# One flat query load with full-width transposes, and gated single-buffered loads, in a pooled-attention plus gated-convolution kernel

## The chip, the cores and the metric

The kernel runs on one core of a Trainium2 chip. The metric is the device time of one execution in microseconds (us). The engines that matter are TensorE (PE in the profile; PEld is its loading of stationary operands), VectorE (DVE), ScalarE (ACT), GpSimd (POOL, which also issues the loads that turn float32 into bfloat16) and SyncE (SP, which issues the other transfers). Matmul results go to an accumulator memory, PSUM, which the kernel uses as four slots.

## The reference

There are 8 batches, 8 heads, 576 tokens and 64 values per head. Keys and values are averaged over 8 neighbouring tokens, which leaves 72 of them. Attention runs over those, and a gated feed-forward block follows.

```python
k_p = k.reshape(B, H, 72, 8, 64).mean(axis=3)
v_p = v.reshape(B, H, 72, 8, 64).mean(axis=3)
attn = softmax(q @ k_p.T / 8)              # per head: 576 x 72
x = (attn @ v_p), heads side by side       # B x 576 x 512
h = maximum(x @ w_in, 0)                   # B x 576 x 1024
c = conv_w[0]*h[t-1] + conv_w[1]*h[t] + conv_w[2]*h[t+1]
out = (h * sigmoid(c)) @ w_out             # B x 576 x 512
```

## The kernel before, in words

The order of every engine's instructions is the order in which the program is written: `start()` does the attention of batch 0, and `batch(b)` then mixes the feed-forward work of batch `b` with the attention of batch `b + 1`, in nine pieces `a0` to `a8` that `attention()` returns. A batch's feed-forward is eight blocks of `mm1` (L246, x times a 128-column block of w_in, ReLU on ACT), four of `conv` (L272, 48 small 32x32 matmuls, then tanh on ACT), four of `gate` (L299, DVE), and four or five of `mm2` (L311, 128 tokens of two batches' output).

The attention of a batch has these steps.

- `k_tree` and `v_tree` (L140, L134) sum eight tokens on DVE by three additions. `k_turn` (L151) transposes the pooled keys on PE and DVE copies them out of PSUM.
- `q_prep(b, h0, n)` (L164) turns the queries of four heads. A row of the query tile holds four neighbouring tokens of a head, so that 128 rows hold tokens 0 to 511; the 64 tokens left lie in a second tile `qt` of 16 rows. Each head takes two transposes of 128x128 (L171) whose result is written in four runs of 32 elements, and two of 16 rows (L174). One DVE copy (L180) takes four heads out of PSUM.
- `scores` (L186) is two matmuls of a head and one exponential on ACT (L197). `av` (L205) multiplies 128 tokens of all heads by the values, and DVE divides by the sum (L220, L221).
- `xt` (L229) transposes the result, with `perm` or `perm_last` in place of the identity matrix, so that tokens come out in their natural order, and DVE copies it (L244). `mm1` needs it.

Every `mm1` block but two is also written a second time with its rows turned by 32, 64 or 96 partitions, by two transfers on SP (L269, L270); `gate` reads those copies.

Loads: the first batch's keys come as float32 through SP, everything else through POOL. Key, value and query tiles have two buffers each; `load(b + 2)` stands in the first piece of `batch(b)`. A load into a buffer in use waits on POOL until its readers are done.

## Time and profile before

| | |
|---|---|
| median of 2 runs | 276.54 us (276.31 to 276.78) |
| profiled execution | 276.06 us, of which the span is 274.2 us |
| PE busy | 243.9 us (89% of the span) |
| DVE busy | 158.7 us (58%) |
| ACT busy | 121.2 us (44%) |
| POOL busy | 33.9 us (12%) |
| moved by DMA | 33.87 MB, 124 GB/s on average |

The profiled execution lies 0.48 us below the median. It spends 1.9 us outside the span. A row of the timeline gives a start and a length in us from the span's start. The length of a group of matmuls holds the pipeline's tail, about a sixth to a fifth of a us; the pace of a series is read from the start of one group to the start of the next. "PEclk" is the clock that TensorE was granted: 1.00 is full, 0.50 half.

### The profile page before, as it was taken

The page shows a single profiled execution, that of the slowest core. Times are in us where ns is not written, and L with a number is a line of the kernel's source. Part 1 is how long each engine was busy: PE and PEld are TensorE (multiplying, and loading weights), DVE is VectorE, ACT ScalarE, POOL GpSimd, SP SyncE. Part 2 cuts the span into 40 slices and gives each one's busy share as a digit, 9 for nine tenths or more (in the row PEclk, how much of TensorE's full clock was granted, in tenths as well). Part 3 has the DMA queues.
Part 4 walks back from the last instruction along what each step waited for, and adds up shares of the span by engine and source line. Part 5 has one row for each costly group of instructions (what it writes and reads, how often), then busy time and mean ns, then how long its engine had stood idle before and what let it go on. Part 6 is the DMA issues. An engine that isn't in the chain of part 4 may idle for free.

```text
span 274.2 us, 7517 instructions
## 1 busy us (share of the span) xinstructions
PE 243.9 (89%) x3244; PEld 157.8 (58%) x3265; DVE 158.7 (58%) x295; ACT 121.2 (44%) x209; POOL 33.9 (12%) x56
## 2 busy tenths in 40 slices
PE   0268889789999999999999999999999999999984
PEld 0145557466666656566666666666666666665531
DVE  3564936484579337664579348664876474742341
ACT  1033016705582346514582358434572638265530
POOL 8452343100220022000220021000000000000000
PEclk9999999959999979997999999999999999999999
DMA  6999999993599229942599229521121212324333
GB/s 132 204 196 186 162 164 200 194 171 67 74 196 211 67 42 167 186 130 65 70 191 202 85 41 196 162 79 47 62 82 62 83 60 82 104 67 130 91 114 117
DMA packets 38045, 33.87 MB, mean 124 GB/s; under 512 B 5732, under 2 KB 32828, under 8 KB 38012
## 3 DMA queue, kind: packets, MB, share of 16 engines
q0 software_dynamic: 24512, 15.68, 42.7%
q1 hardware_dynamic: 13500, 17.72, 21.6%
q8 instruction: 25, 0.41, 0.7%
q14 instruction: 8, 0.07, 0.1%
HBM read 32.52 MB, written 9.44 MB: 153 GB/s over the span
## 4 chain that ended last, share of the span: by engine, by line
PE 65%; ACT 14%; DVE 9%; DMA 6%; issue 4%; POOL 0%; DVEq 0%; ACTq 0%; SPq 0%; POOLq 0%
PE o_ps L317 22%; PE h_ps L251 19%; PE q_ps L171 8%; PE q_ps L174 5%; ACT tg L294 4%; ACT attnT L197 4%; PE c_ps L285 4%; DMA qr<-in_q_dram 4%; DVE x L221 3%; DMA hT_108<-hT_108 3%; ACT hT_108 L259 2%; ACT hT_109 L259 2%; PE sc_ps L189 2%; PE xt_ps L237 2%; PE kT_ps L155 1%
## 5 line engine op out<-in xcount | busy, mean ns | idle before, releaser
L251 PE MATMUL h_ps<-xT,w_in_sb 128*128 128x288 bf16 x512 | 78.0, 298 | 3.1 <-DVE x L221 1.2
L317 PE MATMUL o_ps<-w_out_sb,gT 128*128 128x512 bf16 x267 | 65.6, 382 | 2.1 <-DVE gT L304 0.8
L251 PEld LDWEIGHTS <-w_in_sb 128*128 128x128 bf16 x512 | 49.6, 101 | 21.6 <-issue 4.0
L197 ACT ACTIVATE attnT<-sc_ps 72x576 bf16<-72x576 f32 x64 | 37.8, 651 | 28.7 <-PE sc_ps L189 28.7
L317 PEld LDWEIGHTS <-gT 128*128 128x128 bf16 x288 | 28.0, 99 | 30.2 <-DVE gT L304 1.3
L259 ACT ACTIVATE hT_108<-h_ps 128x576 bf16<-128x576 f32 x32 | 21.0, 656 | 45.2 <-PE h_ps L251 45.1
L259 ACT ACTIVATE hT_109<-h_ps 128x576 bf16<-128x576 f32 x32 | 20.9, 654 | 43.5 <-PE h_ps L251 43.4
L294 ACT ACTIVATE tg<-c_ps 128x576 bf16<-128x576 f32 x64 | 38.3, 661 | 0.2 <-PE c_ps L285 0.2
L180 DVE COPY qT<-q_ps 128x1152 bf16<-128x1152 bf16 x16 | 12.1, 758 | 36.3 <-PE q_ps L174 36.3
L171 PE MATMUL q_ps<-ident,qr 128*128 128x128 bf16 x128 | 30.7, 240 | 2.0 <-DMA qr<-in_q_dram 1.7
L221 DVE TENSOR_TENSOR x<-av_ps,r 128x512 bf16<-128x512 f32 x40 | 27.6, 691 | 1.4
L327 DVE COPY o<-o_ps 128x512 f32<-128x512 f32 x20 | 13.8, 692 | 19.2 <-PE o_ps L317 19.2
L174 PE MATMUL q_ps<-ident,qt 16*128 16x16 bf16 x128 | 23.1, 180 | 0.0
L325 ACT COPY o<-o_ps 128x512 f32<-128x512 f32 x16 | 9.4, 585 | 29.7 <-PE o_ps L317 23.1
L285 PEld LDWEIGHTS <-dw 32*32 32x32 bf16 x1536 | 14.0, 88 | 11.0 <-issue 7.3
L174 PEld LDWEIGHTS <-qt 16*128 16x128 bf16 x128 | 11.8, 92 | 11.7 <-issue 2.5
L210 PEld LDWEIGHTS <-attnT 72*128 72x128 bf16 x320 | 13.8, 104 | 5.9 <-DVE x L221 2.2
L117 POOL DMA_DIRECT2D qt<-in_q_dram x8 | 4.4, 556 | 94.2 <-PE q_ps L174 93.1
L171 PEld LDWEIGHTS <-qr 128*128 128x128 bf16 x128 | 12.6, 98 | 4.3 <-DMA qr<-in_q_dram 1.9
L237 PEld LDWEIGHTS <-x 128*128 128x128 bf16 x160 | 12.1, 108 | 5.0 <-DVE x L221 3.4
L189 PE MATMUL sc_ps<-qT,kz_104 128*72 128x288 bf16 x64 | 12.6, 336 | 1.7 <-DVE qT L180 1.7
L220 DVE RECIPROCAL r<-av_ps 128x8 f32<-128x8 f32 x40 | 8.0, 199 | 8.5 <-PE av_ps L210 8.5
(165 smaller groups left out, 224.3 us busy)
## 6 DMA issues: line engine op xcount, KB each, us to landing
out_dram<-o SPq DMA_DIRECT2D x36, 256.0 KB, 3.7
kr<-in_k_dram POOLq DMA_DIRECT2D x7, 576.0 KB, 13.7
vr<-in_v_dram POOLq DMA_DIRECT2D x7, 576.0 KB, 10.5
qr<-in_q_dram POOLq DMA_DIRECT2D x7, 512.0 KB, 6.6
hT_108<-hT_108 SPq DMA_DIRECT2D x16, 108.0 KB, 4.6
hT_109<-hT_109 SPq DMA_DIRECT2D x16, 108.0 KB, 4.7
hT_108<-hT_108 SPq DMA_DIRECT2D x16, 72.0 KB, 3.9
hT_109<-hT_109 SPq DMA_DIRECT2D x16, 72.0 KB, 2.0
```

Source lines behind the costliest of these rows:

```text
L171: nc.tensor.transpose(out=ym[:, f], in_=st[b]["q"][:, h0 + i, f * P:(f + 1) * P], identity=ident)
L174: nc.tensor.transpose(out=yt[:, f], in_=st[b]["qt"][:, h0 + i, f * P:(f + 1) * P], identity=ident[0:TP, 0:TP],)
L189: nc.tensor.matmul(out=ps[0:Sp, c2, 0:SC], lhsT=kz[b % 2][:, h, c2, :], rhs=st[b]["qT"][h], start=True, stop=True,)
L197: nc.scalar.activation(out=at.rearrange("s (m two j) -> s two m j", two=2, j=GRP), in_=ps[0:Sp, :, 0:SC].rearrange("s two (m j) -> s two m ...
L210: nc.tensor.matmul(out=ps[:, h // 4, c:c + D + 1], lhsT=st[b]["at"][h][:, t0:t0 + P], rhs=va[b % 2][:, h, :], start=True, stop=True,)
L221: nc.vector.tensor_tensor(out=x.rearrange("p (g h) d -> p g h d", g=2), in0=y[:, :, :, 0:D], in1=r.unsqueeze(3).to_broadcast([P, 2, 4, D]) ...
L237: nc.tensor.transpose(out=y[:, pr, ii * P:(ii + 1) * P], in_=st[b]["x"][i][:, 2 * pr:2 * pr + 2, :].rearrange("p h d -> p (h d)"), identit ...
L251: nc.tensor.matmul(out=ps[:, c, 0:SC], lhsT=w_in_sb[:, dc, fb * P:(fb + 1) * P], rhs=xT[:, dc, c * SC:(c + 1) * SC], start=(dc == 0), stop ...
L259: nc.scalar.activation(out=row[:, PAD:S + PAD].rearrange("p (c n) -> p c n", c=NS), in_=ps[:, :, 0:SC], func=ACT.Relu, scale=0.5,)
L285: nc.tensor.matmul(out=ps[j // 2][QD * c:QD * (c + 1), j % 2, 0:SC], lhsT=dw[QD * r:QD * (r + 1), kk, g * NQ + j, :], rhs=row[QD * r:QD * ...
L294: nc.scalar.activation(out=tg[:, 2 * i:2 * i + 2, :], in_=ps[i][:, :, 0:SC], func=ACT.Tanh)
L317: nc.tensor.matmul(out=ps[:, 0, :], lhsT=gT[:, fb, j * P:(j + 1) * P], rhs=w_out_sb[:, fb, :], start=(fb == 0), stop=(fb == n_fb - 1),)
```

## The change

- The queries of a batch are one tile of 128 rows: row `h * 16 + g` holds the 36 tokens from `36 * g` on of head `h`, a contiguous piece of the input. One load brings them, and 18 transposes of 128x128, each for two tokens of every row and so for all heads, turn them, nine in each of two PSUM slots. The copy out of PSUM (L165 in the new numbering) sorts them by head, in runs of 16 elements.
- Every head now needs both halves of the transposes, so the scores leave `a1`; `a2`, `a3` and `a4` have three, three and two heads instead of two each.
- Tokens stand in the attention in the order (token in a row, row): the exponential writes runs of 16 elements instead of 32. The transposes in `xt` write their result in 16 runs of 8 elements, and one `perm` serves all tiles.
- Key, value and query tiles have one buffer each. A batch's loads are written just behind the last reader of the batch before: `load_q` behind the second `q_prep`, `load_v` behind `v_tree`, `load_k` behind `k_tree`, through `pool_keys`.
- In `start()` all loads go through POOL. A one-element copy on POOL, `landed(...)`, stands ahead of most of them, and reads what an earlier load brings, so that POOL waits there for that landing. The scores of the first four heads come behind both halves of `q_prep`, and both `v_tree` behind all scores.
- `first_batch()` takes the place of `batch(0)`: four blocks of `mm1` come ahead of the attention of batch 1, and the second half of the convolution of batch 0 is done there and not in `batch(1)`. `batch(1)` has `pool_keys(2)` in its first piece.
- The output tile has 6 buffers instead of 3, the tanh tile 3 instead of 2.

The diff, cut to what the steps below touch:

```diff
-    kv_pool = ctx.enter_context(tc.tile_pool(name="kv", bufs=2))
-    q_pool = ctx.enter_context(tc.tile_pool(name="q", bufs=2))
+    kv_pool = ctx.enter_context(tc.tile_pool(name="kv", bufs=1))
+    q_pool = ctx.enter_context(tc.tile_pool(name="q", bufs=1))
...
-    tg_pool = ctx.enter_context(tc.tile_pool(name="tg", bufs=2))
-    o_pool = ctx.enter_context(tc.tile_pool(name="o", bufs=3))
+    tg_pool = ctx.enter_context(tc.tile_pool(name="tg", bufs=3))
+    o_pool = ctx.enter_context(tc.tile_pool(name="o", bufs=6))
...
-    q_view = "h (p f) d -> p h (f d)"
+    q_view = "h (g r) d -> (h g) (r d)"
...
+    def load_k(b, h0, n):
+        if h0 == 0:
+            st[b] = {"k": kv_pool.tile([Sp, H, POOL, D], BF16, name="kr")}
+        nc.gpsimd.dma_start(
+            out=st[b]["k"][:, h0:h0 + n], in_=k[b, h0:h0 + n].rearrange(kv_view, p=POOL)
+        )
...
+    def load_q(b):
+        st[b]["q"] = q_pool.tile([P, NI, 2 * D], BF16, name="qr")
         nc.gpsimd.dma_start(
-            out=st[b]["q"][:, h0:h0 + n], in_=q[b, h0:h0 + n, 0:SM].rearrange(q_view, f=4)
-        )
-
-    def load(b):
-        load_k(b)
-        load_q(b, 0, H)
-        load_v(b, 0, H)
+            out=st[b]["q"].rearrange("p i x -> p (i x)"), in_=q[b].rearrange(q_view, g=QG)
+        )
+
+    def landed(ap):
+        nc.gpsimd.tensor_copy(out=seen, in_=ap)
...
-    def q_prep(b, h0, n):
-        ps = slot16("q_ps")
+    def q_prep(b, i0, n):
+        ps = slot16("q_ps").rearrange("d b x -> d (b x)")
         for i in range(n):
-            y = ps[:, i // 2, (i % 2) * SC:(i % 2 + 1) * SC]
-            ym = y[:, 0:SC - GRP].rearrange("d (t f j) -> d f t j", f=2, j=GRP)
-            yt = y[:, SC - GRP:SC].rearrange("d (f j) -> d f j", f=2)
-            for f in range(2):
-                nc.tensor.transpose(
-                    out=ym[:, f], in_=st[b]["q"][:, h0 + i, f * P:(f + 1) * P], identity=ident
-                )
-                nc.tensor.transpose(
-                    out=yt[:, f],
-                    in_=st[b]["qt"][:, h0 + i, f * P:(f + 1) * P],
-                    identity=ident[0:TP, 0:TP],
-                )
-        qT = qT_pool.tile([P, H // 2, SC], BF16, name="qT")[:, 0:n]
+            nc.tensor.transpose(
+                out=ps[:, i * P:(i + 1) * P], in_=st[b]["q"][:, i0 + i, :], identity=ident
+            )
+        if i0 == 0:
+            st[b]["qT"] = qT_pool.tile([P, H, NI, QG], BF16, name="qT")
         nc.vector.tensor_copy(
-            out=qT.rearrange("d (b h) n -> d b (h n)", h=2), in_=ps[:, 0:n // 2, 0:2 * SC]
-        )
-        for i in range(n):
-            st[b].setdefault("qT", {})[h0 + i] = qT[:, i, :]
+            out=st[b]["qT"][:, :, i0:i0 + n, :].rearrange("d h i g -> d i h g"),
+            in_=ps[:, 0:n * P].rearrange("d (i h g) -> d i h g", h=H, g=QG),
+        )
...
-                rhs=st[b]["qT"][h],
+                rhs=st[b]["qT"][:, h].rearrange("d i g -> d (i g)"),
...
-            out=at.rearrange("s (m two j) -> s two m j", two=2, j=GRP),
-            in_=ps[0:Sp, :, 0:SC].rearrange("s two (m j) -> s two m j", j=GRP),
+            out=at.rearrange("s (i two g) -> s two i g", two=2, g=QG),
+            in_=ps[0:Sp, :, 0:SC].rearrange("s two (i g) -> s two i g", g=QG),
...
-        w = len(tiles) * P
-        y = ps[:, 0, 0:n_pairs * w].rearrange("p (c n) -> p c n", c=n_pairs)
+        w = len(tiles) * RT
+        y = ps[:, 0, 0:n_pairs * QG * w].rearrange("p (c g r) -> p c g r", c=n_pairs, g=QG)
         for ii, i in enumerate(tiles):
             for pr in range(n_pairs):
                 nc.tensor.transpose(
-                    out=y[:, pr, ii * P:(ii + 1) * P],
+                    out=y[:, pr, :, ii * RT:(ii + 1) * RT],
                     in_=st[b]["x"][i][:, 2 * pr:2 * pr + 2, :].rearrange("p h d -> p (h d)"),
-                    identity=perm_last if i == 4 else perm,
+                    identity=perm,
                 )
-        n0 = tiles[0] * P
-        skip = n0 - tok0[tiles[0]]
-        nc.vector.tensor_copy(out=st[b]["xT"][:, :, n0:n0 + w - skip], in_=y[:, :, skip:w])
+        r0 = tiles[0] * RT
+        skip = r0 - tok0[tiles[0]] // QG
+        nc.vector.tensor_copy(
+            out=st[b]["xT"].rearrange("p c (g r) -> p c g r", g=QG)[:, :, :, r0:r0 + w - skip],
+            in_=y[:, :, :, skip:w],
+        )
...
+        nc.vector.tensor_copy(
+            out=perm.rearrange("p (g r) -> p r g", r=RT),
+            in_=ident.rearrange("p (r g) -> p r g", r=RT),
+        )
...
     def start():
         nc.sync.dma_start(out=cw_rows, in_=moe_conv_w.rearrange("k (fb p) -> (k fb) p", p=P))
-        load_k_half(0, HH)
-        load_k_half(HH, HH)
-        load_q(0, 0, HH)
+        st[0] = {}
+        load_k(0, 0, HH)
+        load_q(0)
         make_identity(nc, ident)
-        load_v(0, 0, HH)
-        load_q(0, HH, HH)
         make_identity(nc, ident32)
-        load_v(0, HH, HH)
+        load_k(0, HH, HH)
         for i in range(2):
             nc.vector.memset(kz[i], 0.0)
             nc.vector.memset(va[i][:, :, D], float(POOL))
-        for i in range(4):
-            load_w_in(i, 4)
-        for i in range(2):
             nc.gpsimd.memset(hT[i][:, :, :, 0:PAD], 0.0)
             nc.gpsimd.memset(hT[i][:, :, :, S + PAD:S + 2 * PAD], 0.0)
+        landed(st[0]["k"][0:1, 0, 0, 0:1])
+        load_v(0, 0, HH)
+        landed(st[0]["q"][0:1, 0, 0:1])
+        load_v(0, HH, HH)
+        landed(st[0]["k"][0:1, HH, 0, 0:1])
+        load_w_in(0, 4)
+        landed(st[0]["v"][0:1, 0, 0, 0:1])
+        load_w_in(1, 4)
+        landed(st[0]["v"][0:1, HH, 0, 0:1])
+        load_w_in(2, 4)
+        load_w_in(3, 4)
+        landed(w_in_sb[0:1, 0, d_ff // 4:d_ff // 4 + 1])
+        load_k(1, 0, H)
+        landed(w_in_sb[0:1, 0, d_ff - 1:d_ff])
+        load_q(1)
+        landed(st[1]["k"][0:1, 0, 0, 0:1])
+        load_v(1, 0, H)
+        landed(st[1]["q"][0:1, 0, 0:1])
+        for j in range(NQ):
+            load_w_out(j)
         build_conv_w()
         build_perm()
         k_tree(0, 0, HH)
         k_turn(0, 0, HH)
-        q_prep(0, 0, HH)
-        load(1)
-        load_w_out()
-        v_tree(0, 0, HH)
+        q_prep(0, 0, NI // 2)
+        q_prep(0, NI // 2, NI // 2)
         for i in range(HH):
             scores(0, i)
         k_tree(0, HH, HH)
         k_turn(0, HH, HH)
-        q_prep(0, HH, HH)
         for i in range(HH, H):
             scores(0, i)
+        v_tree(0, 0, HH)
         v_tree(0, HH, HH)
         for i in range(4):
...
         def a0():
             k_turn(n, 0, H)
-            q_prep(n, 0, HH)
+            q_prep(n, 0, NI // 2)
 
         def a1():
-            scores(n, 0)
-            scores(n, 1)
-            q_prep(n, HH, HH)
+            q_prep(n, NI // 2, NI // 2)
+            if n + 1 < B:
+                load_q(n + 1)
 
         def a2():
-            scores(n, 2)
-            scores(n, 3)
+            for h in range(3):
+                scores(n, h)
             v_tree(n, 0, H)
+            if n + 1 < B:
+                load_v(n + 1, 0, H)
 
         def a3():
-            scores(n, 4)
-            scores(n, 5)
+            for h in range(3, 6):
+                scores(n, h)
 
         def a4():
-            scores(n, 6)
-            scores(n, 7)
-            if n + 1 < B:
-                k_tree(n + 1, 0, H)
+            for h in range(6, H):
+                scores(n, h)
...
+    def pool_keys(n):
+        if n < B:
+            k_tree(n, 0, H)
+            if n + 1 < B:
+                load_k(n + 1, 0, H)
+
     order = [1, 2, 3, 0, 5, 6, 7, 4]
+
+    def first_batch():
+        att = attention(1)
+        mm1(0, order[0])
+        mm1(0, order[1])
+        mm1(0, order[2])
+        pool_keys(1)
+        mm1(0, order[3])
+        att[0]()
+        mm1(0, order[4])
+        conv(0, 0, 0)
+        att[1]()
+        gate(0, 0, 0)
+        mm1(0, order[5])
+        conv(0, 0, 1)
+        att[2]()
+        gate(0, 0, 1)
+        mm1(0, order[6])
+        att[3]()
+        mm1(0, order[7])
+        att[4]()
+        conv(0, 1, 0)
+        att[5]()
+        gate(0, 1, 0)
+        conv(0, 1, 1)
+        att[6]()
+        gate(0, 1, 1)
+        att[7]()
+        att[8]()
...
     def batch(b):
         att = attention(b + 1) if b + 1 < B else [lambda: None] * 9
-        tiles = [] if b == 0 else list(range(4)) if b % 2 else list(range(4, 9))
+        tiles = list(range(4)) if b % 2 else list(range(4, 9))
 
         def tile_out():
             if tiles:
                 mm2(b - 1, tiles.pop(0))
 
         mm1(b, order[0])
-        if b:
+        if b > 1:
             conv(b - 1, 1, 0)
-        if b + 2 < B:
-            load(b + 2)
+        else:
+            pool_keys(2)
         att[0]()
-        if b:
+        if b > 1:
             gate(b - 1, 1, 0)
 
         mm1(b, order[1])
-        if b:
+        if b > 1:
             conv(b - 1, 1, 1)
         att[1]()
-        if b:
+        if b > 1:
             gate(b - 1, 1, 1)
...
         att[4]()
+        pool_keys(b + 2)
         gate(b, 0, 0)
...
         start()
-        k_tree(1, 0, H)
-        for b in range(B):
+        first_batch()
+        for b in range(1, B):```

The order of instructions at three places, as the built programs have it. First PE, where the queries of a batch are turned in the middle of the program: before, with `qr` the 128-row tile and `qt` the 16-row tile,

```order
L155 MATMUL kT_ps<-ident,kdup 128x72
L171 LDWEIGHTS qr
L171 MATMUL q_ps<-ident,qr 128x4x32
L174 LDWEIGHTS qt
L174 MATMUL q_ps<-ident,qt 128x16
```

and now:

```order
L148 MATMUL kT_ps<-ident,kdup 128x72
L160 LDWEIGHTS qr
L160 MATMUL q_ps<-ident,qr 128x128
L160 LDWEIGHTS qr
L160 MATMUL q_ps<-ident,qr 128x128
```

The pair of shapes, eight times in each half, has become one shape nine times in each half, and its result is one run of 128 elements.

Second ACT, in one batch of the steady part (`attnT` is the exponential, `tg` the tanh, `hT` the ReLU of `mm1`, `o` a copy of `mm2`): before,

```order
L259 ACTIVATE hT_108<-h_ps 128x576
L294 ACTIVATE tg<-c_ps 128x576 x2
L197 ACTIVATE attnT<-sc_ps 72x2x9x32 x2
L259 ACTIVATE hT_108<-h_ps 128x576
L197 ACTIVATE attnT<-sc_ps 72x2x9x32 x2
L259 ACTIVATE hT_108<-h_ps 128x576
L325 COPY o<-o_ps 128x512
L197 ACTIVATE attnT<-sc_ps 72x2x9x32 x2
L259 ACTIVATE hT_108<-h_ps 128x576
L294 ACTIVATE tg<-c_ps 128x576 x2
L197 ACTIVATE attnT<-sc_ps 72x2x9x32 x2
```

and now:

```order
L246 ACTIVATE hT_108<-h_ps 128x576
L281 ACTIVATE tg<-c_ps 128x576 x2
L246 ACTIVATE hT_108<-h_ps 128x576
L181 ACTIVATE attnT<-sc_ps 72x2x18x16 x3
L246 ACTIVATE hT_108<-h_ps 128x576
L312 COPY o<-o_ps 128x512
L181 ACTIVATE attnT<-sc_ps 72x2x18x16 x3
L246 ACTIVATE hT_108<-h_ps 128x576
L281 ACTIVATE tg<-c_ps 128x576 x2
L181 ACTIVATE attnT<-sc_ps 72x2x18x16 x2
```

Two exponentials that stood ahead of the second ReLU here have moved behind the third and the fourth, one to each.

Third POOL, at the program's start (`kr`, `qr`, `vr` are the tiles of keys, queries and values; the second load of each is its second half of heads or the next batch): before,

```order
L118 DMA qr<-in_q_dram 128x4x256
masks.py:197 MEMSET ident_95 32x32
masks.py:199 AFFINE_SELECT ident_95<-ident_95 32x32 [waits Pool_49]
L109 DMA vr<-in_v_dram 72x4x512
L332 DMA w_in_sb<-in_moe_w_in_dram 128x4x256 x3
L332 DMA w_in_sb<-in_moe_w_in_dram 128x4x256 [waits DMASW0_49]
```

and now:

```order
L118 COPY seen<-kr 1x1 [waits DMASW0_49]
L107 DMA vr<-in_v_dram 72x4x512
L118 COPY seen<-qr 1x1 [waits DMASW1_49,Pool_49]
L107 DMA vr<-in_v_dram 72x4x512
L118 COPY seen<-kr 1x1 [waits DMASW2_49,Pool_49]
L319 DMA w_in_sb<-in_moe_w_in_dram 128x4x256
L118 COPY seen<-vr 1x1 [waits DMASW3_49,Pool_49]
L319 DMA w_in_sb<-in_moe_w_in_dram 128x4x256
```

Where before a value load and the four pieces of w_in were issued in a row, each now stands behind a copy that waits for an earlier load.

More of the change, by code (lines that the diff above doesn't have):

```diff
@@ L34 @@
     P = 128
-    SM = 4 * P
-    TP = (S - SM) // 4
+    QG = P // H
+    QR = S // QG
+    NI = QR // 2
+    RT = P // QG
     SC = 288
@@ L73 @@
     perm = const_pool.tile([P, P], BF16)
[L74 removed]
+    seen = const_pool.tile([1, 1], BF16)
     w_in_sb = const_pool.tile([P, n_dmc, d_ff], BF16)
@@ L517 @@
         start()
-        k_tree(1, 0, H)
-        for b in range(B):
+        first_batch()
+        for b in range(1, B):
             batch(b)
```

39 lines of the change are left out of this document (7 added, 32 removed).

## The prediction

> **What bounds the kernel now.** I read the page first, then the stretches of one batch each (from one first `mm1` to the next), then the timeline and the chain of waits inside the stretches. The page's busy times and its chain, by engine:
>
> ```profile
> PE 243.9 (89%) x3244; PEld 157.8 (58%) x3265; DVE 158.7 (58%) x295; ACT 121.2 (44%) x209; POOL 33.9 (12%) x56
> PE 65%; ACT 14%; DVE 9%; DMA 6%; issue 4%; POOL 0%; DVEq 0%; ACTq 0%; SPq 0%; POOLq 0%
> ```
>
> The stretches: length, then busy time of PE, PEld, DVE, ACT and POOL, granted clock, DMA share and GB/s. The first is `start()`, the second batch 0, then batches 1 and 4.
>
> ```profile
> 0.00:32.37 32.37, 15.97 (x118) 10.82 (x119) 18.47 (x49) 5.79 (x9) 15.23 (x32) 1.00 1.23 177
> 32.37:61.43 29.06, 25.20 (x277) 17.40 (x276) 17.66 (x31) 11.29 (x20) 7.04 (x10) 0.89 1.30 181
> 61.43:90.46 29.03, 28.07 (x403) 18.59 (x406) 18.80 (x34) 14.39 (x25) 3.11 (x4) 1.00 0.72 132
> 152.31:182.46 30.15, 29.43 (x411) 19.20 (x413) 18.75 (x33) 15.56 (x27) 2.29 (x3) 1.00 0.53 115
> ```
>
> From 61 us on PE works all but about 1 us of a batch of 30, while DVE has 11 us to spare and ACT 15. What PE sheds there, the kernel gains, as far as DVE and ACT can follow. The first 61 us are another regime: PE is idle for half of the first stretch, and DMA is full in both (177 and 181 GB/s). There the gain is read from who waits for what.
>
> **The query transposes, in batches 1 to 6.** PE's timeline, one half of the queries of a batch and the `mm1` behind it, and eight transposes of `xt` with the `mm1` behind them:
>
> ```profile
> 188.98 0.22 PE L171 MATMUL q_ps<-ident,qr 128*128 128x128 bf16 x1
> 189.12 0.18 PE L174 MATMUL q_ps<-ident,qt 16*128 16x16 bf16 x1
> ...
> 191.15 1.03 PE L251 MATMUL h_ps<-xT,w_in_sb 128*128 128x288 bf16 x7
> 177.84 0.61 PE L237 MATMUL xt_ps<-perm,x 128*128 128x128 bf16 x8
> 178.46 1.15 PE L251 MATMUL h_ps<-xT,w_in_sb 128*128 128x288 bf16 x8
> ```
>
> A half holds PE for 191.15 - 188.98 = 2.17 us, a batch for 4.34. The new transpose has the shape of the `xt` row and writes, like it, one run of 128 elements: 0.62 / 8 = 0.0775 us each, 18 x 0.0775 = 1.40 us. PE sheds 2.94 us per batch, 17.6 us in six.
>
> **What DVE and ACT give back.** The chain through batch 4, where ACT holds it, and the rows of the work that shifts:
>
> ```profile
> 169.31 0.59 ACT tg L294 x2
> 169.89 0.35 issue
> 170.25 0.85 ACT attnT L197 x2
> 170.25 1.20 ACT L197 ACTIVATE attnT<-sc_ps 72x576 bf16<-72x576 f32 x2
> 180.00 1.47 DVE L244 COPY xT<-xt_ps 128x1024 bf16<-128x1024 bf16 x3
> 182.30 1.14 PE L251 MATMUL h_ps<-xT,w_in_sb 128*128 128x288 bf16 x8
> ```
>
> ACT is the chain from `a3` to `a5`, where ReLU, two tanh and the exponentials come denser than PE needs them. The change puts a third exponential in front of that stretch in `a3` (1.20 / 2 = 0.60 us). I let all of it reach PE: 6 x 0.6 = 3.6 us back; nothing would be back if the slack ahead of `a3` takes it. The scores themselves can wait: they moved from `a1` to `a2`, one `mm1` and one `mm2` behind the second copy of the queries.
>
> The DVE copies out of PSUM keep their element counts but write runs of 16 (the last one of 4). I cost them at nothing more. Before the next batch's first `mm1` the three `xT` copies end at 181.47 us and `mm1` starts at 182.30, so 0.83 us cover them, under an `mm2`. What a slower pace would do is a rival below.
>
> **The clock.** Three stretches of 3.4 us in batches 2 and 3, and what stands on PE's timeline ahead of and behind the second half of the queries of batch 2:
>
> ```profile
> 95.80:99.20 3.40, 3.34 (x69) 2.13 (x37) 0.70 (x1) 2.72 (x5) 0.00 (x0) 1.00 0.20 43
> 99.20:102.60 3.40, 3.18 (x12) 1.72 (x13) 1.88 (x3) 0.65 (x1) 1.47 (x2) 0.50 0.30 34
> 126.50:129.90 3.40, 3.40 (x60) 1.99 (x59) 1.80 (x3) 1.37 (x3) 0.00 (x0) 0.50 0.00 1
> 96.23 0.68 PE L189 MATMUL sc_ps<-qT,kz_105 128*72 128x288 bf16 x4
> 99.14 2.07 PE L251 MATMUL h_ps<-xT,w_in_sb 128*128 128x288 bf16 x8
> ```
>
> PE was busy throughout the first stretch, two thirds of it with query transposes, and had half the clock (0.50) in the next; its `mm1` takes 2.07 us there against 1.15. The third stretch is the same again. Each costs half of 3.4 us, 3.4 us together. With fewer transposes there is less to set it off; with an emptier batch 0 there may be more. I take half, 1.7 us, and keep 0 and 3.4. The Trainium skill ("TensorE: Matmul & The Clock Gate", Part 4) says that transposes do not count as busy for the clock gate; the two rows agree, and by that rule the whole 3.4 us would come back.
>
> **The start.** The chain of waits holds the query load; then PE's and DVE's timeline up to the first `mm1`:
>
> ```profile
> 1.95 10.58 DMA qr<-in_q_dram
> 24.25 2.27 ACT attnT L197 x4
> 12.58 0.29 PE L171 MATMUL q_ps<-ident,qr 128*128 128x128 bf16 x1 [1.71 <-DMA qr<-in_q_dram]
> 16.21 2.08 PE L189 MATMUL sc_ps<-qT,kz_104 128*72 128x288 bf16 x8 [0.85 <-DVE qT L180]
> 19.64 0.42 PE L155 MATMUL kT_ps<-ident,kdup 72*128 72x72 bf16 x4 [1.35 <-DVE kdup L143]
> 27.93 1.34 PE L237 MATMUL xt_ps<-perm,x 128*128 128x128 bf16 x8
> 29.06 0.65 PE L210 MATMUL av_ps<-va_106,attnT 72*128 72x65 bf16 x8
> 32.37 2.08 PE L251 MATMUL h_ps<-xT,w_in_sb 128*128 128x288 bf16 x8
> 15.40 0.76 DVE L180 COPY qT<-q_ps 128x1152 bf16<-128x1152 bf16 x1 [3.85 <-PE q_ps L174]
> ```
>
> Half of the queries lands at 12.5 us, and the last exponential ends at 26.5, 5.85 us ahead of the first `mm1`. Now the first keys and all queries are the first two loads: 288 and 576 KB, 0.88 MB (a load of all keys has 576 KB, by its row below), which at the 177 GB/s of the first stretch is 5.0 us. With 3.5 us for issue, first data and completion (my allowance) I put the landing at 8.5; the bounds are 7.5 and, as now, 12.5. From the landing on: 18 transposes at the slow pace of the start, (29.06 - 27.93) / 8 = 0.14, are 2.5; copy 0.76; four scores 2.1; transposes of the second keys 0.42, and their two copies, at most 0.76; four scores 2.1; last exponential 0.6; then 5.85 as now. That is 15.1, and the first `mm1` comes at 23.6, 8.8 us earlier, or 4.8 with the late landing. The values must land by 17 us; they are the fourth and fifth load, and 1.77 MB up to their end take 10.0 us at 177 GB/s, 13.5 with the allowance. I take 8.0, for gaps between gated loads.
>
> **Batch 0.** From the chain of waits: one `k_tree` and the longest wait of batch 0, then a convolution of batch 4; from the list of waits, DVE's at a gate; DVE's timeline:
>
> ```profile
> 32.71 1.14 DVE t_383 L129
> 33.87 0.70 DVE t_385 L131
> 34.59 0.70 DVE kdup L143
> 45.93 7.19 DMA hT_108<-hT_108
> 153.28 0.66 PE c_ps L285 x48
> DVE gT L304 <- DMA hT_108<-hT_108: 3.1, 1, 3.1
> 54.11 0.69 DVE L221 TENSOR_TENSOR x<-av_ps,r 128x512 bf16<-128x512 f32 x1
> ```
>
> `gate` waits for a turned copy that takes 7.19 us beside the loads of two batches, and holds DVE, hence `av` and PE; 3.1 us of it are idle time of DVE. Fewer loads are in flight now: 3.1 us gained, from none of it to all. The query transposes give 2.9. Against it, the second half of the convolution adds 2 x 0.66 = 1.3 on PE, and with no `mm1` left behind `av`, PE waits for the last `x`, a gate and the `xT` copies: 0.69 + 1.2 + 1.47 less what is there today, about 2 us. Net 2.7 us gained (from -2 to 6). Batch 1 loses that convolution, 1.3, but has `pool_keys(2)` in its first piece: 2.5 us of DVE (1.14 + 0.70 + 0.70) against one `mm1` of 1.1, so PE waits about 1.5. Net 0.2 lost. Loads sit on POOL behind their readers, one batch ahead of use, some 25 us; the slowest took 13.7 us at the median:
>
> ```profile
> kr<-in_k_dram POOLq DMA_DIRECT2D x7, 576.0 KB, 13.7
> ```
>
> So the single buffers cost nothing in the steady part. Behind a waiting `landed` on POOL stand only further loads.
>
> **Sum.** 17.6 - 3.6 + 1.7 + 8.0 + 2.7 - 0.2 = 26.2 us from the profiled 276.06: 249.9. The median is 0.48 above that execution: 250.3 us.
>
> **The rivals.**
>
> *PSUM written in short runs is slow; slower than before.* The `xt` transposes of four tiles in five, 16 per batch, 128 in all, now write 16 runs of 8 elements with gaps. The trace has one gapped form, the 128x4x32 of the queries: from its start to that of the next matmul 189.12 - 188.98 = 0.14 us pass, against 0.0775 for one run (I allow 0.16, as a pair takes 2.17 / 8 = 0.27 on average). For that extra of up to 0.083 speaks the gap; against it, that the next matmul loads a 16-row operand, and that the change of shape explains it too. If it is the gaps, 0.083 for each of 128 is 10.6 us: 260.9. If it is so much per run (0.028 for each of three more), 15 more runs cost 0.415, 53 us in all: 303. The point of no gain is 26.2 / 128 = 0.205 us each. The Trainium skill ("PSUM — Partial Sum Buffer", Specifications) says that any non-contiguous pattern slows matmuls significantly; that is this rival, it gives no figure, and the row of the queries neither shows nor excludes it.
>
> *DVE copies at half pace.* If runs of 16 cost DVE the pace of its float32 row (0.69 us for 512 elements), the three `xT` copies take 1.6 us more, 0.8 beyond their cover: 6 x 0.8 and twice 1.6 at the start, 8 us: 258.3.
>
> *Gated loads starve the start.* Two short loads in flight may not fill the DMA queues that today run at 177 GB/s. If the start gains nothing and batch 0 neither, 10.7 us are gone: 261. For it: each gate adds POOL's issue to the chain; against it: before, the queues held loads that nobody needed for 30 us.
>
> **Chances and range.** Forecast 0.65; slow DVE copies 0.12; gaps at 0.083 0.09; starved start 0.07; both of the last two, about 271, 0.03; slower 0.04. All but the last two are faster by over 2% (a limit of 271.0, and about what a measurement can tell from no change): faster 0.93, same 0.03, slower 0.04. The forecast's own range is 242 to 258: all upper ends at once (no loss to ACT, 3.4 of clock, 8.8 and 6 at the start) give 241, all lower ends (no clock, 4.8 and -2) 260. To hold 8 in 10 it takes in the middle rivals at 258 to 261: 240 to 261.
>
> **What would show it.** Right: a half of `q_ps` of 0.7 us on PE, batches of some 27.5 us, the first `mm1` near 24 us, ACT in more of the chain. Wrong: an `xt` group of eight above 0.62 us (gaps), an `xT` copy above 0.68 (DVE), POOL's copies waiting past 20 us for v or w_in with PE idle (starved), batches still near 30 with PE idle before `av` (ACT).

## The result and the profile after

The changed kernel takes 249.14 us (median of 247.42 and 250.87) against 276.54: a ratio of 0.901, 95% interval 0.874 to 0.928. Timed once more in four executions beside seven of the kernel before (277.07), it takes 251.13 us, ratio 0.905 (0.898 to 0.913). The forecast was 250.3 us, in a range of 240 to 261. The profiled execution is the one of 247.42 us, with a span of 245.7. Here and below, a ratio compares only executions in the faster of the two states in which one kernel can run, so it can differ a little from the quotient of two medians.

The page of the kernel after, busy times and the chain of waits by engine:

```profile
PE 218.3 (89%) x3153; PEld 142.7 (58%) x3153; DVE 156.9 (64%) x287; ACT 121.3 (49%) x209; POOL 30.9 (13%) x58
PE 62%; ACT 15%; DVE 11%; DMA 5%; issue 5%; POOL 0%; DVEq 0%; SPq 0%; ACTq 0%; POOLq 0%
```

PE has lost 25.6 us of busy time and is still busy for 89% of a shorter span. The stretches of the kernel after, with the columns of the prediction's table (length, busy time of PE, PEld, DVE, ACT and POOL, granted clock, DMA share, GB/s): the start, batches 0 and 1, batches 4 and 5, and the stretch of half clock.

```profile
0.00:24.24 24.24, 12.41 (x103) 9.54 (x104) 17.30 (x42) 5.80 (x9) 10.64 (x30) 1.00 0.92 130
24.24:51.96 27.72, 21.66 (x358) 15.04 (x358) 17.34 (x32) 13.82 (x24) 9.06 (x14) 0.89 1.08 183
51.96:80.15 28.19, 26.85 (x294) 17.79 (x294) 18.87 (x32) 12.09 (x21) 3.05 (x4) 0.86 0.80 150
132.88:159.95 27.07, 26.47 (x400) 17.32 (x399) 18.66 (x33) 15.54 (x27) 2.23 (x3) 1.00 0.71 149
159.95:185.62 25.67, 24.83 (x392) 16.50 (x390) 19.27 (x34) 14.37 (x25) 1.43 (x2) 1.00 0.55 124
46.00:59.70 13.70, 9.06 (x58) 6.32 (x59) 10.49 (x19) 1.30 (x2) 1.18 (x2) 0.50 0.85 131
```

Measured in the same way, from the first `mm1` of a batch to the next, the 28.5 us of span went like this (us; batch 1 of before ends at 90.29, a little ahead of the end that the prediction's row took):

| stretch | before | after | gained | predicted |
|---|---|---|---|---|
| start | 32.37 | 24.24 | 8.13 | 8.0 |
| batch 0 | 29.06 | 27.72 | 1.34 | 2.7 |
| batch 1 | 28.86 | 28.19 | 0.67 | 2.1 |
| batches 2 to 6 | 150.98 | 132.53 | 18.45 | 13.4 |
| batch 7 and end | 32.90 | 32.97 | -0.07 | 0 |

(Predicted, batch 1: 2.94 - 0.6 - 0.2. Batches 2 to 6: five times 2.94 - 0.6, and 1.7 of clock.) Nearly two thirds of the gain lie in the steady part, where PE's work changes only in the queries. The first two batches gave less than predicted.

PE's timeline of the kernel after, half of the queries of batch 2 with the `mm1` behind it, and eight transposes of `xt` with the `mm1` behind them:

```profile
82.16 0.67 PE L160 MATMUL q_ps<-ident,qr 128*128 128x128 bf16 x9
82.67 1.14 PE L238 MATMUL h_ps<-xT,w_in_sb 128*128 128x288 bf16 x8
102.76 0.61 PE L221 MATMUL xt_ps<-perm,x 128*128 128x128 bf16 x8
103.37 1.15 PE L238 MATMUL h_ps<-xT,w_in_sb 128*128 128x288 bf16 x8
```

A half holds PE for 82.67 - 82.16 = 0.51 us, where it held it for 2.17. The `xt` transposes, now written in 16 runs of 8 elements, have a group of eight at 0.61 us, as before.

### The profile page after: what moved, and what is told of

It is laid out like the page before. It is cut to its first block, busy times and chain, and to the rows that moved or that the text cites. A ratio compares the mean times of both kernels' runs of the same rounds, so it can differ in the third digit from the quotient of the medians.

```text
span 245.7 us, 7301 instructions
## 1 busy us (share of the span) xinstructions
PE 218.3 (89%) x3153; PEld 142.7 (58%) x3153; DVE 156.9 (64%) x287; ACT 121.3 (49%) x209; POOL 30.9 (13%) x58
## 4 chain that ended last, share of the span: by engine, by line
PE 62%; ACT 15%; DVE 11%; DMA 5%; issue 5%; POOL 0%; DVEq 0%; SPq 0%; ACTq 0%; POOLq 0%
PE o_ps L304 25%; PE h_ps L238 22%; ACT attnT L181 5%; PE q_ps L160 4%; PE c_ps L272 4%; ACT tg L281 4%; DVE x L205 3%; DVE o L314 3%; DMA qr<-in_q_dram 3%; DMA hT_108<-hT_108 3%; ACT hT_108 L246 3%; ACT hT_109 L246 2%; PE xt_ps L221 2%; PE kT_ps L148 1%; ACT o L312 1%
## 5 line engine op out<-in xcount | busy, mean ns | idle before, releaser
L238 PE MATMUL h_ps<-xT,w_in_sb 128*128 128x288 bf16 x512 | 77.3, 298 | 5.1 <-DVE xT L228 2.3
L304 PE MATMUL o_ps<-w_out_sb,gT 128*128 128x512 bf16 x288 | 67.1, 379 | 0.8 <-DVE gT L291 0.8
L238 PEld LDWEIGHTS <-w_in_sb 128*128 128x128 bf16 x512 | 50.6, 101 | 25.3 <-issue 7.9
L181 ACT ACTIVATE attnT<-sc_ps 72x576 bf16<-72x576 f32 x64 | 37.2, 655 | 19.1 <-PE sc_ps L173 19.1
L304 PEld LDWEIGHTS <-gT 128*128 128x128 bf16 x288 | 27.8, 98 | 29.5 <-DVE gT L291 1.3
L246 ACT ACTIVATE hT_109<-h_ps 128x576 bf16<-128x576 f32 x32 | 21.0, 656 | 44.5 <-PE h_ps L238 44.5
L281 ACT ACTIVATE tg<-c_ps 128x576 bf16<-128x576 f32 x64 | 38.4, 664 | 0.6 <-PE c_ps L272 0.6
L246 ACT ACTIVATE hT_108<-h_ps 128x576 bf16<-128x576 f32 x32 | 21.0, 657 | 24.9 <-PE h_ps L238 24.9
L205 DVE TENSOR_TENSOR x<-av_ps,r 128x512 bf16<-128x512 f32 x40 | 27.7, 692 | 1.4
L312 ACT COPY o<-o_ps 128x512 f32<-128x512 f32 x16 | 9.4, 586 | 29.5 <-PE o_ps L304 29.5
L272 PEld LDWEIGHTS <-dw 32*32 32x32 bf16 x1536 | 14.1, 88 | 11.5 <-issue 8.0
L221 PE MATMUL xt_ps<-perm,x 128*128 128x128 bf16 x160 | 15.1, 236 | 5.9 <-DVE x L205 3.9
L221 PEld LDWEIGHTS <-x 128*128 128x128 bf16 x160 | 11.5, 104 | 8.6 <-DVE x L205 7.0
L113 POOL DMA_DIRECT2D qr<-in_q_dram x8 | 4.9, 617 | 81.9 <-PE q_ps L160 79.9
L165 DVE COPY qT<-q_ps 128x1152 bf16<-128x1152 bf16 x16 | 12.1, 756 | 4.8 <-PE q_ps L160 4.5
L173 PE MATMUL sc_ps<-qT,kz_104 128*72 128x288 bf16 x64 | 12.2, 326 | 1.2 <-DVE qT L165 0.8
L160 PE MATMUL q_ps<-ident,qr 128*128 128x128 bf16 x144 | 12.5, 243 | 0.7 <-DMA qr<-in_q_dram 0.7
L272 PE MATMUL c_ps<-hT_108,dw 32*32 32x288 bf16 x768 | 12.0, 287 | 0.8 <-ACT hT_108 L246 0.5
L228 DVE COPY xT<-xt_ps 128x1024 bf16<-128x1024 bf16 (+1 forms) x24 | 12.0, 548 | 0.1
```

What stands on the lines that cost most here:

```text
L160: nc.tensor.transpose(out=ps[:, i * P:(i + 1) * P], in_=st[b]["q"][:, i0 + i, :], identity=ident)
L173: nc.tensor.matmul(out=ps[0:Sp, c2, 0:SC], lhsT=kz[b % 2][:, h, c2, :], rhs=st[b]["qT"][:, h].rearrange("d i g -> d (i g)"), start=True, s ...
L181: nc.scalar.activation(out=at.rearrange("s (i two g) -> s two i g", two=2, g=QG), in_=ps[0:Sp, :, 0:SC].rearrange("s two (i g) -> s two i ...
L205: nc.vector.tensor_tensor(out=x.rearrange("p (g h) d -> p g h d", g=2), in0=y[:, :, :, 0:D], in1=r.unsqueeze(3).to_broadcast([P, 2, 4, D]) ...
L221: nc.tensor.transpose(out=y[:, pr, :, ii * RT:(ii + 1) * RT], in_=st[b]["x"][i][:, 2 * pr:2 * pr + 2, :].rearrange("p h d -> p (h d)"), id ...
L238: nc.tensor.matmul(out=ps[:, c, 0:SC], lhsT=w_in_sb[:, dc, fb * P:(fb + 1) * P], rhs=xT[:, dc, c * SC:(c + 1) * SC], start=(dc == 0), stop ...
```

## The experiments

Each run is given by its edit, the expectations, and what came. "First `mm1` of batch 2" sums up all that lies ahead of the steady part: 90.29 us before, 80.15 after. The stretches are of one profiled execution each.

### The whole change once more

> The changed kernel once more, beside the kernel before on the same chip, for a narrower ratio and a second look at the clock. Its two runs so far are 247.4 and 250.9 us at granted clocks of 0.969 and 0.95; if the half clock in batch 1 makes that difference, the times scatter over 247 to 251 and go with the clock.

251.13 us (249.37 to 252.62), ratio 0.905. First `mm1` of batch 0 at 24.27, of batch 2 at 81.54; batches 3 to 6 as in the first profile, within 0.6 us. What varies lies in batch 0 (29.76 here, 27.72 there) and 1. The times do not go with the clock: the longest, 252.62, had 0.964, the shortest, 249.37, had 0.959.

### The query load alone

The kernel before, with the flat load, the 18 transposes, the new token order and the scores in threes; loads, two buffers, start and batch 0 in the order of before.

```diff
-    q_view = "h (p f) d -> p h (f d)"
+    q_view = "h (g r) d -> (h g) (r d)"
...
-        q_prep(0, 0, HH)
+        q_prep(0, 0, NI // 2)
+        q_prep(0, NI // 2, NI // 2)
...
-            q_prep(n, HH, HH)
+            q_prep(n, NI // 2, NI // 2)
```

> The kernel before with the flat query load, the 18 transposes, the new token order and the scores in three pieces alone; loads, buffers, start and batch 0 stay as before. Theory: the steady gain is PE's shed transposes and nothing else, so batches 2 to 6 take 25.7 and 27.1 us as in the changed kernel, batch 0 loses some 3, and the start stays within 1 us of 32.4: 251 to 255 us in all. Rival: the steady gain needs the later, single-buffered loads too (less traffic beside the turned copies); then the batches stay above 28 us and the time above 258.

245.35 us (244.59 to 247.41), ratio 0.886 (0.879 to 0.893): 5.8 us faster than the whole change. Batches 2 to 6 are 27.06, 25.67, 27.06, 25.67, 27.06 us after the change and 27.07, 25.71, 27.06, 25.72, 27.06 here: the steady part is the query load and nothing else. The expectation for the start was wrong, and the time lies below the one expected. PE's timeline of this run:

```profile
10.22 2.10 PE L164 MATMUL q_ps<-ident,qr 128*128 128x128 bf16 x18 [0.79 <-DMA qr<-in_q_dram]
27.58 2.08 PE L242 MATMUL h_ps<-xT,w_in_sb 128*128 128x288 bf16 x8 [0.38 <-DVE xT L232]
```

All queries land at 10.2 us, where the first half landed at 12.5, and the first `mm1` comes 4.8 us earlier, without any gate. Of the 8.1 us at the start, 3.3 are left for the new loads and the new order in `start()`. (From start to start a transpose takes 0.107 us here and 0.056 in batch 2: PE runs at half its pace at the start, although the clock column reads 1.00 there.)

### The old transposes in another order

The kernel before, with nothing but the order of the transposes in a half changed: eight of 128 rows first, then the eight of 16 rows.

```diff
         for i in range(n):
             ...
             for f in range(2):
                 nc.tensor.transpose(out=ym[:, f], ...)
-                nc.tensor.transpose(out=yt[:, f], ...)
+        for i in range(n):
+            ...
+            for f in range(2):
+                nc.tensor.transpose(out=yt[:, f], ...)
```

> The kernel before, with the same transposes in another order: in each half the eight of 128 rows (written in four runs of 32) first, the eight of 16 rows behind them. Theory: it is the change between the two shapes that makes a pair take 0.27 us; in groups each transposes at 0.055 us or less, so a half takes some 0.9 us in place of 2.17 and the kernel 257 to 260 us. Rival 1: the gaps in the output cost it; the eight then take 0.16 us each, a half stays near 2 us and the kernel at 274 to 277. Rival 2: the 16-row transposes are slow by themselves (0.11 us each): a half 1.3 us, the kernel near 264.

252.15 us (251.1 to 252.98), ratio 0.908 (0.901 to 0.916). With the same loads, the same 32 transposes and the same gapped writes, this order alone gains 25 us. That is 5 us below the lowest time expected, and within 1 us of the whole change (251.13, with intervals that overlap). PE's timeline of this run, one half in the steady part:

```profile
192.34 0.61 PE L170 MATMUL q_ps<-ident,qr 128*128 128x128 bf16 x8
192.89 0.35 PE L177 MATMUL q_ps<-ident,qt 16*128 16x16 bf16 x8
193.18 1.16 PE L254 MATMUL h_ps<-xT,w_in_sb 128*128 128x288 bf16 x8
```

The eight large ones, in four runs of 32 elements, hold PE for 0.55 us, the eight of 16 rows for 0.29: a half of 0.84 in place of 2.17. Twice the difference is 2.66 us per batch, and batch 6 is 2.69 shorter than before (27.47 against 30.16). Beyond that, the first `mm1` comes at 29.15 us, 3.2 earlier, and batches 2 and 3, which lost their half clock, are 4.3 and 3.9 shorter. The flat load takes the half from 0.84 to 0.51 and the batch to 27.06.

### The same alternation with full operands

The kernel before with its order tile by tile, but the second tile kept in 128 rows (zeros below the 16), so that every transpose is 128x128.

```diff
...
-                    out=yt[:, f],
+                    out=ps[:, i // 2, c0 + f * TP:c0 + f * TP + P],
                     in_=st[b]["qt"][:, h0 + i, f * P:(f + 1) * P],
-                    identity=ident[0:TP, 0:TP],
+                    identity=ident,
```

> The kernel before with the same alternation of query transposes, tile by tile, but with the 16-row tile kept in 128 rows (112 of them zero, set once in the first microseconds), so that every transpose is 128x128; the surplus columns are overwritten or not read. Two theories of what the alternation costs. If it is the change of the number of rows of the operand, 16 transposes at 0.055 to 0.07 us make a half of about 1.0 us in place of 2.17, a batch is some 2.3 us shorter (28 and 26.5 us), and the kernel comes to about 256 us. If it is the alternation as such (two tiles in turn, a gapped result and a run in turn), a half stays at 2.1 us or more and the time at 276 to 279 us.

253.27 us (252.94 to 254.89), ratio 0.922 (0.915 to 0.928). PE's timeline of this run, one half:

```profile
166.31 0.22 PE L173 MATMUL q_ps<-ident,qr 128*128 128x128 bf16 x1
166.37 0.22 PE L176 MATMUL q_ps<-ident,qt 128*128 128x128 bf16 x1
166.43 0.22 PE L173 MATMUL q_ps<-ident,qr 128*128 128x128 bf16 x1
...
167.15 0.22 PE L176 MATMUL q_ps<-ident,qt 128*128 128x128 bf16 x1
167.21 1.14 PE L253 MATMUL h_ps<-xT,w_in_sb 128*128 128x288 bf16 x8
```

Two tiles in turn, a gapped and a contiguous result in turn, and still one every 0.056 us: 0.90 for the half. Sixteen larger transposes in turn take less than half the time of eight large and eight small ones in turn. So it is not the alternation that is slow, but the turn between an operand of 128 rows and one of 16. This run also makes the second tile's identity matrix and result larger; the last section has a turn in which no identity matrix takes part.

### Without the gates

The changed kernel without the `landed(...)` copies; the loads keep their order.

> The changed kernel without the copies on POOL that wait for landings; same loads in the same order. Theory: the loads of one queue land in the order in which they are issued, so the first keys and queries land when they do now (6.1 and 9.1 us) and the first block of mm1 stays at 24.2 us, with the later loads landing earlier: the time is the same within 2 us. Rival: the loads behind take a share of the bandwidth, as in the kernel before, where half of the queries landed at 12.5 us; then queries land 2 to 4 us later and the first mm1 comes at 26 to 28 us, 2 to 4 us more in all.

247.09 us (246.05 to 248.09), ratio 0.891 (0.885 to 0.897): 4 us below the whole change, with intervals that just fail to touch. Neither expectation had the time fall by that much. The queries land at 9.3 us (9.0 with gates), so the loads behind them take next to nothing from them. The profiled execution, the slowest of its four, shows little of the gain (first `mm1` of batch 0 at 24.52, of batch 2 at 80.83). What it does show is that the keys of batch 1 are there when DVE comes to them. DVE's timeline without gates:

```profile
24.39 1.21 DVE L122 TENSOR_TENSOR t<-kr 72x2048 bf16<-72x2048 bf16 x1
38.02 0.76 DVE L291 TENSOR_TENSOR gT<-tg,hT 128x1152 bf16<-128x1152 bf16 x1 [2.60 <-DMA hT<-hT]
46.44 0.76 DVE L291 TENSOR_TENSOR gT<-tg,hT 128x1152 bf16<-128x1152 bf16 x1 [1.57 <-DMA hT<-hT]
```

and with them:

```profile
27.30 1.22 DVE L122 TENSOR_TENSOR t_399<-kr 72x2048 bf16<-72x2048 bf16 x1 [3.11 <-DMA kr<-in_k_dram]
37.44 0.76 DVE L291 TENSOR_TENSOR gT<-tg_519,hT_108 128x1152 bf16<-128x1152 bf16 x1 [2.65 <-DMA hT_108<-hT_108]
46.07 0.76 DVE L291 TENSOR_TENSOR gT<-tg_738,hT_108 128x1152 bf16<-128x1152 bf16 x1 [1.83 <-DMA hT_108<-hT_108]
```

The waits of `gate` for the turned copies are there either way.

### Batch 0 in the plain order, with and without gates

The changed kernel with `batch(0)` in place of `first_batch()`, `pool_keys(1)` ahead of it; then the same without the gates.

```diff
...
-        first_batch()
-        for b in range(1, B):
+        pool_keys(1)
+        for b in range(B):
...
```

> The changed kernel with batch 0 in the order of all other batches, as in the kernel before; gated single-buffered loads and the new start stay. Theory: the start stays at 24.3 us, but one mm1 ahead of the keys of batch 1, which land at 27.3, leaves PE idle for some 4 us; batch 0 about 28 us without the second convolution, batch 1 25.7: 244 to 248 us. Rival (first_batch hides the late keys and is worth its end): 250 us or more.

> The same without the copies on POOL that wait for landings. This is the query layout alone plus the new start and single buffers. Theory: gates only delay the loads behind them; keys of batch 1 land earlier, and the time is 1 to 4 us below the gated one, 242 to 245 us, below the 245.4 of the query layout alone because the start is 3 us shorter. Rival: without gates the start is longer and it comes out at 246 us or more.

With the gates 252.37 us (251.6 to 254.46), ratio 0.919 (0.903 to 0.935), as the rival had it. Without them 244.84 (244.44 to 245.1), ratio 0.892 (0.882 to 0.902), as the theory had it. DVE's timeline with the gates, the keys of batch 1 and of batch 2; then without:

```profile
29.12 1.22 DVE L122 TENSOR_TENSOR t<-kr 72x2048 bf16<-72x2048 bf16 x1 [4.87 <-DMA kr<-in_k_dram]
50.06 1.22 DVE L122 TENSOR_TENSOR t<-kr 72x2048 bf16<-72x2048 bf16 x1 [10.48 <-DMA kr<-in_k_dram]
```

```profile
24.47 1.21 DVE L122 TENSOR_TENSOR t<-kr 72x2048 bf16<-72x2048 bf16 x1
40.05 1.22 DVE L122 TENSOR_TENSOR t<-kr 72x2048 bf16<-72x2048 bf16 x1 [5.26 <-DMA kr<-in_k_dram]
```

With gates DVE stands for 15.4 us at two loads of keys, without them for 5.3, and the first `mm1` of batch 2 comes at 87.21 and at 77.85. So the gates make the keys late. They cost 7.5 us in this order and 4.0 in the order of `first_batch`, each found between runs on one chip; so `first_batch`, with four `mm1` ahead and `pool_keys(2)` put off, hides part of it. Whether `first_batch` itself pays is not shown: with the gates 251.13 us stand against 252.37, without them 247.09 against 244.84, but on two chips, and the intervals of the ratios overlap both times (0.905 and 0.919, 0.891 and 0.892).

### The end of batch 0

Two other ends of `first_batch`, with all gates kept. First: the second half of convolution and gates goes back to `batch(1)`, the last `mm1` stands between the last two pieces of the attention, `pool_keys(2)` comes behind `a4`, and the w_out loads behind the load of the keys of batch 2. Second: as this, but the convolutions stay in batch 0 and no `mm1` is kept for the end.

```diff
...
-        mm1(0, order[7])
         att[4]()
-        conv(0, 1, 0)
+        pool_keys(2)
         att[5]()
-        gate(0, 1, 0)
-        conv(0, 1, 1)
         att[6]()
-        gate(0, 1, 1)
         att[7]()
+        mm1(0, order[7])
         att[8]()
...
```

> The changed kernel with another end of batch 0: one block of mm1 stands between the last transposes as in every other batch, the second half of the convolution and its gates are back in batch 1, the keys of batch 2 are summed behind the scores, and w_out is loaded behind the keys of batch 2. Theory: the end of batch 0 (gates that wait for turned copies, then PE idle for 5 us and more, then 10 to 14 us at half clock) is what the changed kernel lost against the query layout alone; batches 0 and 1 then take 26 and 26 us in place of 28 to 30 and 28, and the time is 244 to 247 us. Rival: it is the gated loads that hold batch 0; then batch 0 stays at 28 us or more and the time at 249 or more.

> As the run with another end of batch 0, but the second half of the convolution stays in batch 0, between the pieces of av, and only its gates move to batch 1; no mm1 stands in the end. Theory (gates that wait for turned copies are the culprit): as fast as that run, 243 to 247 us. Rival (PE's idle time without an mm1 sets off the half clock whoever waits): 248 us or more, with half clock behind 48 us.

246.79 us (245.36 to 248.39), ratio 0.900 (0.886 to 0.914), and 246.64 (245.86 to 247.58), ratio 0.899 (0.888 to 0.910). Both times lie where they were expected. In the medians both are some 4 us below the repeated whole change, in the ratios about half a per cent (some 1.5 us), and their intervals overlap its own. Their first two batches are 53.24 and 54.49 us, against 55.91. The half clock stays, for 6.8 us in the first (44.1 to 50.9) and 10.2 in the second (45.6 to 55.8), and so do PE's waits for DVE. In the first, PE waits 3.56 us for `x`, behind a DVE that waits 0.90 us for the keys of batch 2 and then sums them; in the second it waits 4.27 us for the values and 3.03 for `x`, behind a DVE that waits 6.56 us for a turned copy. The two don't tell which of the moves pays.

### The two best, side by side

The query load alone, and the whole change in plain order without gates, five rounds each against the same runs of the kernel before (275.7).

> The kernel before with the flat query load alone, once more beside the next run, on the same chip and against the same runs of the kernel before: 245.3 us, ratio 0.886. In the spans it was 1.3 us longer than the next kernel at first look.

> The change without the gates and with the plain order of batch 0, once more: 244.8 us. If its shorter start (24.6 against 27.6 us to the first mm1) is worth something behind batch 1, it is 0.5 to 2 us below the run with the query load alone; if the loads take it back, the two are the same within 0.3%.

246.25 us (245.66 to 248.69), ratio 0.896 (0.891 to 0.902), and 245.32 (244.81 to 245.96), ratio 0.892 (0.887 to 0.897). The start is 2.3 us shorter in the second, and the first `mm1` of batch 2 comes 1.05 us earlier; 0.9 us are left in the medians, and the intervals overlap. Both medians lie below that of the change as made. For the query load alone that was clear in the first run (0.886 against 0.905 on one chip) and is less so here (0.896, with an interval that overlaps the one of the change): by these figures it gains 2 to 6 us more than the whole. Single buffers as such cost nothing here: their steady batches are the same within 0.05 us. They were not tried apart from the order of the loads.

## Why the prediction was right, and where its parts were not

The direction, the size and the places were right. The sum was close partly by luck, because two errors stood against each other: the steady part was put 5.1 us too low, batches 0 and 1 together 2.8 too high.

**Query transposes: too low.** The mechanism held; the size was off. The pace of 0.0775 us was read from eight `xt` transposes to the start of the `mm1` behind them, and held a wait. PEld's timeline of before shows it, at that same `mm1`:

```profile
178.46 0.48 PEld L251 LDWEIGHTS <-w_in_sb 128*128 128x128 bf16 x5 [0.18 <-DVE x L221]
```

Its first operand load stood 0.18 us for DVE's `x`. (0.62 - 0.18) / 8 is 0.055 us, and the half of the kernel after has 0.51 / 9 = 0.057. So PE sheds 2 x (2.17 - 0.51) = 3.32 us per batch, not 2.94. The prediction also took the price to lie in the number of transposes; 2.66 of the 3.32 us are gained with all 32 of them, in another order.

**ACT gives back 0.6 per batch: too much.** Batches 4, 5 and 6 are shorter by 3.09, 3.14 and 3.10 us, of 3.32 shed, so 0.2 came back. The idle time of PE in batch 4 did not grow (30.15 - 29.43 = 0.72 us before, 27.07 - 26.47 = 0.60 after). The 0.2 lie inside PE's busy time, at the scores: from the start of each group of scores of batch 4 to the start of what follows it, 0.74, 0.49, 0.49 and 0.76 us passed before, 2.48 together, and 0.94, 0.83 and 0.96 pass now, 2.73. The profile puts the waits there down to copies and activations of ACT and DVE that had to end first. With the old transposes in groups, and the scores still in twos, the sum is 2.49, and nothing comes back (2.69 of 2.66).

**Clock: half taken, all of it came.** In batches 2 and 3 no stretch of half clock is left, here or in any of the eleven runs above, and those two batches gained 1.7 and 1.2 us beyond the 3.1 of the others, 2.9 of the 3.4. The rule of the Trainium skill ("TensorE: Matmul & The Clock Gate", Part 4), that transposes don't count as busy the same way, agrees with that: the 4.3 us of transposes per batch went down to 1.0 in the kernel after, and to 1.7 or 1.8 in the two experiments that keep 32 of them. But those two experiments keep all the transposes and take away only the time lost at the turns between them, so that lost time explains it as well; no run separates the two, nor why the clock falls there and not elsewhere. Against it, "with an emptier batch 0 there may be more" came true: half clock for 13.7 us around the end of batch 0, where it was 6.8 before. Its length differs between executions of one kernel: the query load alone has 6.8 us in its first profile and none in its second.

**Start: right** (8.13 for 8.0). The queries land at 9.0 us for 8.5, though no row had shown the 3.5 us allowed for issue and completion, and from there to the first `mm1` it takes 15.3 us for 15.1. The step put all of it down to the new order of loads and transposes together; 4.8 of the 8.1 come with the flat load alone, in the load order of before, and 3.2 with nothing but the old transposes in groups.

**Batches 0 and 1: too high.** PE's timeline after, at the seam of the two:

```profile
47.73 0.61 PE L221 MATMUL xt_ps<-perm,x 128*128 128x128 bf16 x4 [2.38 <-DVE x L205]
51.96 2.08 PE L238 MATMUL h_ps<-xT,w_in_sb 128*128 128x288 bf16 x8 [1.94 <-DVE xT L228]
54.54 0.66 PE L148 MATMUL kT_ps<-ident,kdup 72*128 72x72 bf16 x8 [0.50 <-DVE kdup L136]
```

"Fewer loads are in flight now: 3.1 us gained" failed: DVE waits for the turned copies for 2.65 and 1.83 us, 4.5 together (rows above). The traffic in that stretch did not fall (183 GB/s, 181 before), and the waits are nearly the same without gates (2.60 and 1.57), so the gates are not their cause. The two copies that end the waits took 6.4 and 6.7 us to land. The first two of the batch, issued ahead of the loads of the values and of w_out, took 3.4 and 3.0, and in batch 6, with no loads left, the median is 2.2. That speaks for the loads beside them; no run takes these away alone. PE's wait at the end was put at about 2 us and is 2.38 + 1.94. The stall at `pool_keys(2)` is 0.50 us, a third of the 1.5 expected. What batch 1 lost is the clock: from 51.96 to 59.70 it runs at half (`mm1` 2.08 us for eight matmuls, 1.14 at full clock). With the clock full all through batch 1, as in the query load alone, it takes 25.66 us, 2.5 less.

**Gapped PSUM writes: refuted.** Runs of 8 elements in `xt` cost nothing (0.61 us per eight in both kernels), and neither do runs of 32 in the reordered queries (0.055 us from start to start inside the eight; their 0.55 hold the turn behind them). The rule of the Trainium skill ("PSUM — Partial Sum Buffer", Specifications) that any non-contiguous pattern slows matmuls significantly does not hold for these transposes. The row that the rival rested on, 0.14 us from one transpose to the next, was the change of operand.

**DVE copies at half pace: refuted.** DVE's groups by form, the `xT` copy before and after:

```profile
L244 DVE COPY xT<-xt_ps 128x1024 bf16<-128x1024 bf16 x16 | 10.4, 680 | 0.8 <-PE xt_ps L237 0.8
```

```profile
L228 DVE COPY xT<-xt_ps 128x1024 bf16<-128x1024 bf16 x16 | 10.3, 681 | 0.0
```

Runs of 16 elements leave it at 681 ns.

**Gated loads starve the start: no, but they starve what comes next.** The start moves 130 GB/s in place of 177, and POOL waits past 20 us, as the rival's sign would have it, yet PE's first `mm1` has its data. The price falls on the keys of batch 1: 3.11 us of DVE in the row above. The rival had the right mechanism one stage too early, and cost 4 us in the medians and up to 7.5 with the plain order.

## What to carry to other kernels

Look at the order in which TensorE meets operands of few rows (16 and 32 here) among full ones before their number or layout: grouping equal ones was worth 25 us of 277 here, for an edit of a few lines. Read the pace of a series from the starts inside it, or from a row whose follower did not wait. A rewrite that bundles a layout, a load order and a schedule should be split: here one part earned more than the whole.

## What the hardware showed

The turn between operands of 128 and 16 rows was the surprise. Alternating, a half of the queries turns 16 times, with the step to `mm1`; grouped it turns twice. The difference of 1.33 us over 14 turns is 0.095 us each. PE's and PEld's timelines of before, two transposes and their weight loads:

```profile
189.51 0.23 PE L171 MATMUL q_ps<-ident,qr 128*128 128x128 bf16 x1
189.67 0.18 PE L174 MATMUL q_ps<-ident,qt 16*128 16x16 bf16 x1
189.50 0.10 PEld L171 LDWEIGHTS <-qr 128*128 128x128 bf16 x1
189.66 0.09 PEld L174 LDWEIGHTS <-qt 16*128 16x128 bf16 x1
```

and of the kernel with all operands at 128 rows:

```profile
169.74 0.22 PE L176 MATMUL q_ps<-ident,qt 128*128 128x128 bf16 x1
169.80 0.22 PE L173 MATMUL q_ps<-ident,qr 128*128 128x128 bf16 x1
169.74 0.10 PEld L173 LDWEIGHTS <-qr 128*128 128x128 bf16 x1
169.80 0.10 PEld L176 LDWEIGHTS <-qt 128*128 128x128 bf16 x1
```

With equal rows the load of an operand starts 0.06 us ahead of its matmul, together with the matmul before it; with the rows in turn it starts 0.01 us ahead. The load no longer runs beside the transpose before it. That fits the price.

Other turns in the kernel after tell what it goes with. PE's timeline, one `mm1` with a convolution behind it, whose operands are 32x32, and one with `mm2` behind it, of 128 rows:

```profile
82.67 1.14 PE L238 MATMUL h_ps<-xT,w_in_sb 128*128 128x288 bf16 x8
83.74 0.73 PE L272 MATMUL c_ps<-hT_109,dw 32*32 32x288 bf16 x48
84.92 1.14 PE L238 MATMUL h_ps<-xT,w_in_sb 128*128 128x288 bf16 x8
85.90 1.89 PE L304 MATMUL o_ps<-w_out_sb,gT 128*128 128x512 bf16 x8
```

From the start of `mm1` to the start of what follows, 1.07 us pass ahead of the convolution and 0.98 ahead of `mm2`. So the turn to 32 rows costs 0.09 us too, with no identity matrix in it and nothing that the profile shows PE to wait for. PEld starts to load for the convolution only with its first matmul, at 83.74, and for `mm2` 0.12 us ahead, at 85.78. From the keys' transposes (72 rows) to the queries' (128 rows) the price is absent: the load of the first `qr` starts at 82.13 us, 0.03 ahead of its transpose, beside the last of the keys. So it is not every change of the row count. In these traces it is the turn between 16 or 32 rows and 128.
